# One 24-row read of a channel-attention kernel as two reads, of 123 and of 5 partitions

## The chip, the cores and the metric

The kernel runs on one core of a Trainium2 chip. The metric is the time of one execution on the device in microseconds (us). The time before is the median of three runs, 725.32 us (725.16 to 725.88).

## The reference

The input x has 384 x 384 pixels with 384 channels in bf16. The kernel takes the mean and the maximum of every channel over all pixels, sends both through the same small two-layer network (384 to 96 to 384), adds the two results, applies a sigmoid, and multiplies every pixel by the resulting 384 factors.

```python
xf = x.reshape(B, H * W, C)
gap = jnp.mean(xf, 1)
gmp = jnp.amax(xf, 1)
h_a = gap @ w1
h_a = h_a * (h_a > 0)
h_m = gmp @ w1
h_m = h_m * (h_m > 0)
scale = sigmoid(h_a @ w2 + h_m @ w2)
return x * scale[:, None, None, :]
```

So x has to be read once in full before the first output can be written. x has 113 MB and does not fit into the core's memory, which is why most of it is read twice.

## The kernel before, in words

**Rows.** The 147,456 pixels are dealt out over 128 partitions, 1,152 pixels to each. The kernel calls one pixel per partition a row: 768 bytes (384 channels in bf16) in each of 128 partitions. A block is a run of consecutive rows; within it each partition holds consecutive pixels, so that a read of n rows takes one contiguous piece of n x 768 bytes per partition (`rows_of`, line 110). The buffer `body` holds 280 rows, `held` five more.

**First pass.** All 1,152 rows are read by 53 reads that SyncE issues at line 371, in the order of the list `steps` (lines 222 to 256). For each read, TensorE sums the channels (`sums`, line 274) and VectorE takes the running maximum into `acc`, up to six rows at a time (`maximum`, line 340). Seven groups of 32 rows (`packed_block`, parts 0 to 6) stay in the buffer: ScalarE tests their values (lines 301 and 302), and TensorE and ScalarE pack 32 rows into the space of 24 (lines 322 to 329). The other rows of the first pass pass through the low rows of `body`, again and again: `BETWEEN` (line 57) lists, for each part, the blocks that are read after it and the place in `body` that they take. A read waits until the engines have finished with what lay in its place.

Part 4 is read as 24 rows into `homes[4]`, rows 256 to 279 of `body` (line 238, `FIRST_AT[4]` is 200), and 8 rows more (line 239). After it come the four blocks of `BETWEEN[4]`, of 34, 36, 31 and 26 rows, of which the first lies in rows 208 to 241 of `body`. Then part 5 is read, whose 24 rows lie in rows 232 to 255.

**Between the passes.** `fold` (line 352) and the transposes (line 423) reduce the maximum, the small network gives the factors, and ScalarE's sigmoid (line 431) writes them to `scale_bc`.

**Second pass.** What stayed in the buffer is multiplied at line 436 and written out by ScalarE's queue. The other rows are read again (line 529), multiplied and written (lines 445, 451 and 490), while VectorE and ScalarE unpack the packed parts (lines 468 to 487).

**Order.** The order on every engine is written out by hand (`manual_schedule`, line 197). SyncE issues all reads, ScalarE's queue all writes. The semaphores of the transfers are shared round robin among eight. The packed rows are restored without a loss if a test value (`judge`) is zero, else they are read again at the end (line 586); in the profiled execution they are not.

## Time and profile before

| what | value |
|---|---|
| median of three runs | 725.32 us |
| the profiled execution's own time | 725.41 us |
| its span, first to last instruction | 723.6 us |
| VectorE (DVE) busy | 564.1 us, 78% |
| ScalarE (ACT) busy | 349.8 us, 48% |
| TensorE (PE) busy | 184.7 us, 26% |
| moved by DMA | 305.63 MB, 422 GB/s over the span |
| share of 16 DMA engines, reads (q1) and writes (q10) | 62.3% and 36.6% |
| transfers under way at the longest: first pass, from issue to landing | 42.2 us at most, 19.8 in the median |

The page cuts the span into 40 slices of 18.1 us and gives the busy share of each engine in tenths. The DMA row is the mean busy share of the core's 16 DMA engines. An issue of a transfer is a short instruction on its queue; the transfer itself runs on the DMA engines, packet by packet, and is over at its landing, when the last of its end markers has come in. "L340" is line 340 of the kernel. The chain of waits follows the end of the execution back to what released each step.

### The profile page before, as it was taken

The numbers are of one execution on the slowest core, as the hardware profiler recorded it, in microseconds if no ns is written. First come the engines' busy times: TensorE is split into PE (matmuls) and PEld (weight loads), VectorE is DVE, ScalarE is ACT, GpSimd is POOL, SyncE is SP. The second block draws the span as 40 slices with busy tenths as digits, with TensorE's granted clock in tenths as the row PEclk, the third lists the DMA queues.
The fourth block names the chain that finished last, engine by engine and source line by source line (L and its number), as shares of the span: only waits on it lengthen the run. The fifth ranks groups of instructions, "written<-read, shape, count | busy, mean of one in ns | idle before, by whom it ended". The sixth has DMA issues, their size and how long they took to land.

```text
span 723.6 us, 3882 instructions
## 1 busy us (share of the span) xinstructions
PE 184.7 (26%) x1363; PEld 74.2 (10%) x1363; DVE 564.1 (78%) x445; ACT 349.8 (48%) x251; POOL 0.7 (0%) x6
## 2 busy tenths in 40 slices
PE   5577475965867470000000000000000000001000
PEld 1222122322322140000000000000000000001000
DVE  5699899999999998797966554897888889495200
ACT  6999999997999200056230023806154442200000
POOL 0000000000000000000000000000000000000000
PEclk9888878896988555555555555555555555555555
DMA  9999999999999979999999999999999999999997
GB/s 380 434 438 435 417 442 427 429 430 432 431 426 428 426 312 356 400 433 431 433 431 431 434 428 431 434 430 435 430 429 432 437 432 430 430 433 439 442 426 339
DMA packets 20403, 305.63 MB, mean 422 GB/s; under 512 B 2624, under 2 KB 2976, under 8 KB 7200
## 3 DMA queue, kind: packets, MB, share of 16 engines
q1 hardware_dynamic: 13040, 192.14, 62.3%
q10 hardware_dynamic: 7344, 113.25, 36.6%
q8 instruction: 10, 0.16, 0.1%
q14 instruction: 9, 0.07, 0.0%
HBM read 192.14 MB, written 113.25 MB: 422 GB/s over the span
## 4 chain that ended last, share of the span: by engine, by line
DMA 63%; DVE 25%; issue 3%; PE 2%; ACT 1%; SPq 0%; DVEq 0%; ACTq 0%
DMA rows<-in_x_dram 40%; DMA out_dram<-rows 23%; DVE acc L340 16%; DVE rows L436 9%; PE words_ps L322 1%; ACT rows L328 0%; DVE acc L436 0%; SPq L371 0%; PE bank_a L274 0%; ACT rows L329 0%; ACT rows L487 0%; PE bank_a L430 0%; ACT scale_bc L431 0%; DVE small L424 0%; PE bank_a L423 0%
## 5 line engine op out<-in xcount | busy, mean ns | idle before, releaser
L436 DVE TENSOR_TENSOR rows<-rows,scale_bc 128x9216 bf16<-128x9216 bf16 (+9 forms) x56 | 230.9, 4164 | 91.2 <-DMA rows<-in_x_dram 90.0
L340 DVE TENSOR_TENSOR acc<-acc,rows 128x2304 bf16<-128x2304 bf16 (+4 forms) x227 | 245.0, 1154 | 13.9 <-DMA rows<-in_x_dram 13.6
L487 ACT COPY rows<-rows 128x1536 uint8<-128x1536 uint8 x28 | 41.3, 1476 | 204.2 <-DVE rows L436 144.8
L274 PE MATMUL bank_a<-rows,small 128*1 128x512 bf16 (+3 forms) x897 | 93.3, 466 | 80.9 <-DMA rows<-in_x_dram 76.1
L346 PE MATMUL words_ps<-ident_bf,acc 128*128 128x128 bf16 x24 | 2.7, 310 | 376.3 <-DVE acc L574 376.3
L301 ACT ACTIVATE rows<-rows 128x3072 uint8<-128x3072 int8 (+1 forms) x35 | 81.9, 2341 | 9.1 <-DMA rows<-in_x_dram 8.4
L302 ACT ACTIVATE rows<-rows 128x3072 uint8<-128x3072 uint8 (+1 forms) x35 | 82.0, 2344 | 1.1
L487 ACT COPY rows<-acc 128x1536 uint8<-128x1536 uint8 x42 | 60.5, 1473 | 18.2 <-DVE acc L473 17.7
L274 PEld LDWEIGHTS <-small 128*1 128x1 bf16 x897 | 30.6, 95 | 140.3 <-issue 118.2
L346 PEld LDWEIGHTS <-acc 128*128 128x128 bf16 x24 | 2.5, 144 | 376.7 <-DVE acc L574 376.7
L322 PE MATMUL words_ps<-rows,scale_bc 128*128 128x512 fp8e4 (+1 forms) x126 | 37.9, 414 | 9.2 <-ACT rows L329 9.2
L328 ACT COPY rows<-rows 128x1536 uint8<-128x1536 uint8 x28 | 39.7, 1468 | 0.4 <-PE words_ps L322 0.4
L322 PE MATMUL words_ps<-rows 128*128 128x512 fp8e3 (+1 forms) x126 | 35.8, 394 | 0.0
L468 DVE TENSOR_SCALAR rows<-rows 128x1536 uint16<-128x1536 uint16 x56 | 31.3, 560 | 1.9
L322 PE MATMUL words_ps<-rows,w_sb 128*128 128x512 fp8e3 x84 | 27.0, 405 | 0.0
L487 ACT COPY acc<-rows 128x1536 uint8<-128x1536 uint8 x14 | 20.5, 1466 | 0.0
L329 ACT ACTIVATE rows<-words_ps 128x1536 uint16<-128x1536 f32 x14 | 20.1, 1439 | 0.0
L322 PEld LDWEIGHTS <-scale_bc 128*128 128x128 bf16 x126 | 12.2, 103 | 30.2 <-issue 19.3
L322 PEld LDWEIGHTS <-rows 128*128 128x128 bf16 x126 | 12.9, 102 | 16.7 <-issue 3.3
L473 DVE SCALAR_TENSOR_TENSOR acc<-acc,rows 128x768 uint32<-128x768 uint32 x14 | 13.4, 959 | 0.5
L473 DVE SCALAR_TENSOR_TENSOR rows<-rows 128x768 uint32<-128x768 uint32 x14 | 13.4, 958 | 0.5
L284 ACT COPY w_sb<-bank_a 65x128 f32<-65x128 f32 x2 | 0.5, 261 | 24.5 <-PE bank_a L274 24.0
(61 smaller groups left out, 72.0 us busy)
## 6 DMA issues: line engine op xcount, KB each, us to landing
rows<-in_x_dram SPq DMA_DIRECT2D x16, 2880.0 KB, 25.4
out_dram<-rows ACTq DMA_DIRECT2D x15, 2880.0 KB, 22.8
rows<-in_x_dram SPq DMA_DIRECT2D x15, 2304.0 KB, 20.0
out_dram<-rows ACTq DMA_DIRECT2D x14, 2304.0 KB, 21.1
rows<-in_x_dram SPq DMA_DIRECT2D x4, 3072.0 KB, 31.8
out_dram<-rows ACTq DMA_DIRECT2D x2, 4608.0 KB, 46.7
rows<-in_x_dram SPq DMA_DIRECT2D x9, 768.0 KB, 16.7
rows<-in_x_dram SPq DMA_DIRECT2D x2, 3264.0 KB, 26.4
```

Source lines behind the costliest of these rows:

```text
L274: nc.tensor.matmul(sum_ps[q * QP:q * QP + 1, 0:g * P], lhsT=ones_bf[:, 0:1], rhs=rows[:, k:k + g, q * P:(q + 1) * P], start=(done + k == 0 ...
L301: nc.scalar.activation(out=out_, in_=rows, func=ACT.Square, bias=test_bias, scale=TEST_SCALE)
L302: nc.scalar.activation(out=out_, in_=out_, func=ACT.Square, bias=minus4, accum_out=tests[:, k:k + 1],)
L322: nc.tensor.matmul(words[:, c:c + BANK], lhsT=weights[2 * r + k], rhs=high(part(i, r), dt)[:, half * n + c:half * n + c + BANK], start=(r ...
L328: nc.scalar.copy(out=high(part(i, r), U8)[:, span], in_=low(part(i, r + 2), U8)[:, span])
L329: nc.scalar.activation(out=part(i, 2).rearrange("p n c -> p (n c)").bitcast(U16)[:, span], in_=words, func=ACT.Copy, bias=32767.5,)
L340: nc.vector.tensor_tensor(out=out_, in0=in0, in1=in1, op=ALU.max)
L346: nc.tensor.transpose(out=out_[:, r, q * P:(q + 1) * P], in_=rows[:, r, q * P:(q + 1) * P], identity=ident_bf)
L436: nc.vector.tensor_tensor(out=dst, in0=src, in1=scale_bc.unsqueeze(1).to_broadcast([P, n, C]), op=ALU.mult)
L468: nc.vector.tensor_scalar(out=u16(dst), in0=u16(src), scalar1=s1, scalar2=s2, op0=op0, op1=op1)
L473: nc.vector.scalar_tensor_tensor(out=u32(v), in0=u32(v), scalar=0x3F3F3F3F, in1=u32(m), op0=ALU.bitwise_xor, op1=ALU.bitwise_xor)
L487: nc.scalar.copy(out=dst, in_=src)
```

## The change

The first read of part 4, the 24 rows at `FIRST_AT[4]`, is issued as two reads of the same 24 rows: one of partitions 0 to 122, one of partitions 123 to 127. They go to the same place in `body` from the same place in x. All other reads keep a single issue of 128 partitions, and what the engines do with the rows stays as it was.

```diff
+UNEVEN, FIRST_PARTITIONS = 4, 123
...
         _, block, rows, lo, hi = st
         m = hi - lo
-        nc.sync.dma_start(out=rows, in_=rows_of(xr, block)[:, lo:hi, :])
+        parts = (0, P)
+        if block == packed_block and lo == FIRST_AT[UNEVEN]:
+            parts = (0, FIRST_PARTITIONS, P)
+        for a, b in zip(parts, parts[1:]):
+            nc.sync.dma_start(out=rows[a:b], in_=rows_of(xr, block)[a:b, lo:hi, :])
         if nth < len(loads) - SUM_TAIL:
             sums(rows, m, done, TOT - tail_rows)
```

## The prediction

> **What bounds the kernel now.** I read the busy share by slices first, then the table by stretches, then the chain of waits, then a narrow window of the DMA queues for the time of one packet.

> ```profile
> DMA  9999999999999979999999999999999999999997
> GB/s 380 434 438 435 417 442 427 429 430 432 431 426 428 426 312 356 400 433 431 433 431 431 434 428 431 434 430 435 430 429 432 437 432 430 430 433 439 442 426 339
> ```

> The DMA engines are full in all but two slices (about 260 to 280 us, between the passes). The table by stretches says it without rounding; the last two columns are DMA share and GB/s.

> ```profile
> 120.00:140.00 20.00, 12.88 (x99) 4.90 (x101) 18.89 (x18) 19.42 (x13) 0.00 (x0) 0.83 1.00 426
> 140.00:160.00 20.00, 15.78 (x117) 6.41 (x110) 20.00 (x20) 19.81 (x14) 0.00 (x0) 1.00 1.01 433
> ...
> 220.00:240.00 20.00, 13.56 (x96) 5.11 (x96) 19.71 (x20) 19.82 (x15) 0.00 (x0) 0.76 1.01 430
> 240.00:260.00 20.00, 10.76 (x76) 3.14 (x76) 19.13 (x20) 0.19 (x1) 0.00 (x0) 0.50 1.01 425
> 260.00:270.00 10.00, 8.43 (x95) 6.13 (x95) 9.93 (x11) 0.95 (x4) 0.00 (x0) 0.50 0.69 268
> 270.00:280.00 10.00, 2.41 (x38) 1.69 (x34) 7.82 (x12) 0.83 (x3) 0.00 (x0) 0.50 0.76 265
> ```

> From 120 to 260 us the share is 0.99 to 1.01: no DMA engine has time to spare in the rest of the first pass. VectorE is nearly full too (18.9 to 20.0 of 20), so the chain of waits changes sides:

> ```profile
> 102.06 24.16 DMA rows<-in_x_dram
> 126.21 0.03 issue
> ...
> 164.08 20.67 DMA rows<-in_x_dram
> ...
> 230.38 11.09 DMA rows<-in_x_dram
> 241.47 0.03 issue
> ```

> At 126.2, 184.8 and 241.5 VectorE stood waiting for a landing. So up to 241.5 it has no backlog that a pause could work off to the kernel's gain; what comes after (small reads, folds, the scale) follows that landing at a fixed distance. A DMA engine that is late in the first pass makes the kernel as late.

> The time of a packet, from the window 134:136 us, inside the read in question:

> ```profile
> DMA packets 46, 0.85 MB, mean 424 GB/s; under 512 B 0, under 2 KB 0, under 8 KB 0
> ...
> q1 hardware_dynamic: 46, 0.85, 98.6%
> ```

> 46 packets took 98.6% of 16 engines times 2 us: 0.686 us each. A packet is the 18,432 B (24 rows of 768 B) of one partition. The page's second line of queues counts 2,624 packets under 512 B: 384 are the pieces of w1, and the other 2,240 are 16 end markers for each of 140 transfers. So each transfer runs on all 16 engines, 8 of 128 partitions on each (6 of w2's 96).

> **The change, part by part.** In the order of the built instructions SyncE has one more; nothing else moves, apart from semaphores that go round one further.

> Removed: one 128-partition read, 8 x 0.686 = 5.49 us of every engine.

> Added, first: one more issue on SyncE, 0.33 to 0.56 us by line 371's rows. The split read is issued at 109.45 and lands 29.6 us later, so that time lies under the queue; uncovered it costs 0.4 us. Behind it stands the 8-row read (landing after 30.9 us), covered as well.

> Added, second: 123 partitions. Every transfer of this trace is cut into 16 equal shares of whole partitions. 123 = 3 x 41 has no such cut; the largest number of engines up to 16 that takes equal shares is 3, with 41 partitions each. [...] The three engines then have 41 x 0.686 = 28.1 us, and 0.7 us more for a partition of the other read: 28.8 us in place of 5.5, **+23.3 us**, if a packet keeps its time.

> Does it? While the three engines work on it, the other thirteen have the next five reads of the queue: 8, 34, 36, 31 and 26 rows, all issued by 142.9 us into rows that reads ahead of the split one leave free. That is 135 rows at 5.49/24 = 0.229 us, 30.9 us of work. Those thirteen write to their own partitions, and the three now write to the same ones at the same time. No row shows two engines on the same partitions. From below: 0.686 us holds for packets of this size in reads and writes alike (median of both directions in the packet records), as if the engine alone set the pace. From above: both halve, 1.37 us. The longest single packet of this size took 1.18 us. I take half pace for as long as the thirteen have work, since each group of 8 partitions receives 26.9 GB/s from its one engine in all full stretches, never more, and the core's 442 GB/s at most is 16 times 27.6: I see no headroom for a second writer. Then 30.9 us bring 15.4 us of the work, the other 13.4 us run at full pace: 44.3 us in place of 5.5, **+38.8 us**. Half pace to the end: 57.6 in place of 5.5, +52.1.

> [...]

> Does the queue run dry behind it? The next read after those five waits until VectorE has passed the 34-row block (it lies over the same rows of the buffer). When the three engines end the split read, they have the 8 and 34 rows next (9.6 us), then VectorE needs 34 x 0.215 = 7.3 us (245.0 us for about 1,141 rows in line 340's group); the issue comes at 17 us, and 36 + 31 + 26 rows keep the engines to 30.9 us. Not dry; all that follows keeps its spacing, carried by the three late engines.

> A small credit: the transfer before the last stretch of the chain lands with its last marker at 241.47, while the middle of its 16 markers is near 239.7. A late trio need not hold the slowest engine; the last of three drawn from these markers is at about 240.2. **-1.3 us** (0 to -3.2).

> Sum against the profiled execution, 725.41 us (span 723.6 and 1.8 around it), and 0.09 above the median of the runs: 725.3 + 38.8 - 1.3 = **763 us**. The second pass, after the fixed distance, is shifted whole.

> **The rivals.**
> - Three engines, but each keeps 0.686 us: 725.3 + 23.3 - 1.3 = 747 us. For it: the packet time is the same in every full stretch. Against: no stretch has two engines on the same partitions.
> - Not slower: the transfer is dealt out unevenly over all 16 engines, fifteen with 8 partitions and one with 3, and the five others go to five engines. For it: all 140 transfers have 16 markers. Against: all have multiples of 16. If the short engine is the late one, it gains 5 x 0.686 = 3.4 us and the landing at 241.47 moves to its next marker, 240.2: -1.2 us; if not, one packet more on the late one: +0.7. So 724 to 726 us. It decides as soon as 14 or more engines carry the read (at most 9 partitions each, one over the 8 of before). That the split does nothing is the same case.
> - One engine takes the whole: 123 x 0.686 = 84.4 in place of 5.5: 804 us. For it: an equal cut into a power of two exists for 123 only as 1.
> - The delay is hidden, since reads are issued 20 to 30 us ahead: this speaks against itself, as the queue is FIFO work for engines that are 100% busy, so a longer queue hides no work. I count it with the even deal.

> **Chances.** Half pace 0.45; own pace 0.35; even deal or hidden 0.12; one engine 0.04; something else, slower, 0.04. The range 745 to 777 takes the first two with their bounds (747 less 1.9 for the markers' spread, 725.3 + 52.1 at the top) and leaves the even deal and the one engine out. A measurement of this kernel can tell about 0.2% (1.5 us) from no change: faster 0.03, same 0.09, slower 0.88.

> **What the profile after would show.** Right: DMA share falls to 3/16 = 0.19 from about 133.5 + 31 = 165 us until the next issue, at about 133.5 + 44.3 + 17 = 195; VectorE idle until the landing; the 123-partition read lands some 39 us later after its issue than the 29.6 of before; packets of 18,432 B with 1.37 us among them; the second pass as long as before. Own pace: a hole of half that length (to 133.5 + 28.8 + 17 = 179), a landing 23 us later, and all packets at 0.686. Even deal: no hole, both reads landing about 30 us after issue. Wrong in the step on the queue: the hole repeats further on. Wrong in the step on the end: the time between the last landing and the first multiply changes from its 7.9 us (268.3 to 276.2).

## The result, and the profile after

The changed kernel takes 776.51 us (median, 776.03 to 777.27) beside 725.54 us for the kernel before (four runs, one more than the 725.32 above rests on): 1.0704 times as long (95% interval 1.0685 to 1.0722), 51.0 us more. Its profiled execution took 776.03 us, with a span of 774.2 us. In its profile the read of line 371 is L377 and the running maximum of line 340 is L342.

The same rows of the page as before, and the line of packet counts:

```profile
DMA  9999999998499799699999999999999999999998
GB/s 383 438 424 432 438 430 400 222 218 207 166 391 429 322 402 426 252 396 419 435 432 428 434 434 428 428 431 433 432 434 430 433 433 433 430 433 435 436 432 348
DMA packets 20395, 305.63 MB, mean 395 GB/s; under 512 B 2616, under 2 KB 2968, under 8 KB 7192
```

Packets under 512 B were 2,624 and are 2,616. Sixteen end markers of the read are gone, and eight have come: 3 for the read of 123 partitions and 5 for that of 5. So the shares are as the prediction has them. What it did not have stands in the first two rows together: for three slices (of 19.4 us here, 135 to 194 us) the DMA engines are 9, 9 and 8 tenths busy and move half as much. The table by stretches of the changed kernel (last columns: DMA share, GB/s):

```profile
110.00:130.00 20.00, 11.29 (x82) 4.29 (x83) 18.63 (x18) 19.80 (x15) 0.00 (x0) 0.76 1.00 432
...
142.00:180.00 38.00, 0.00 (x0) 0.00 (x0) 0.86 (x1) 0.00 (x0) 0.00 (x0) 0.50 1.00 217
180.00:187.00 7.00, 0.00 (x0) 0.00 (x0) 0.00 (x0) 0.00 (x0) 0.00 (x0) 0.50 1.03 220
190.00:205.00 15.00, 12.08 (x83) 4.84 (x84) 12.59 (x12) 14.79 (x10) 0.00 (x0) 0.91 0.22 92
215.00:255.00 40.00, 25.64 (x195) 9.71 (x192) 38.52 (x36) 35.75 (x25) 0.00 (x0) 0.84 1.00 413
```

All sixteen engines are busy from 142 to 187 us, and together they move 217 GB/s in place of 432: all at half their pace, not the three alone (of the packets over 4 KB that start from 142 to 187 us, none moved over 16 GB/s, in the median 13.4; from 110 to 130 us it was 27.0). Then three engines are left with their backlog (share 0.22, 92 GB/s; 3/16 would be 0.19 and 81), until the next reads come. The end markers of the reads behind tell the same: of the sixteen of the 34-row read 13 come by 153.2 us and 3 from 197.8 us on, and of the 26-row read, the last in the queue, 13 by 192.2 us and 3 from 219.0 us on. VectorE meanwhile:

```profile
129.75 13.11 DVE L342 TENSOR_TENSOR acc<-acc,rows 128x2304 bf16<-128x2304 bf16 x12
190.15 6.97 DVE L342 TENSOR_TENSOR acc<-acc,rows 128x2304 bf16<-128x2304 bf16 x7 [47.29 <-DMA rows<-in_x_dram]
```

It stands for 47.3 us, for the rows of the one split read. The chain of waits shows the same gap, but under another name:

```profile
135.70 7.16 DVE acc L342 x7
142.86 47.17 another core or an unknown queue
190.15 3.77 DVE acc L342 x4
```

No other core is there. The rows came with the read of 123 partitions (three markers, the last at 188.79 us) and that of 5 (five markers, the last at 190.03 us); elsewhere in this trace a read has sixteen. That the profile leaves the wait without a name for want of markers is likely, but not shown.

From here the delay only travels. The landing at 241.47 us before is at 291.64 (+50.2), the last landing of the pass 318.63 for 268.33 (+50.3), the first multiply 326.6 for 276.2 (+50.4), and from there to the end it is 447.6 us for 447.4.

### The profile page after: what moved, and what is told of

Its sections match the earlier page's. It is cut to its first block, busy times and chain, and to the rows that moved or that the text cites. A ratio compares the mean times of both kernels' runs of the same rounds, so it can differ in the third digit from the quotient of the medians.

```text
span 774.2 us, 3883 instructions
## 1 busy us (share of the span) xinstructions
PE 184.2 (24%) x1363; PEld 73.8 (10%) x1363; DVE 564.3 (73%) x445; ACT 349.9 (45%) x251; POOL 0.7 (0%) x6
## 4 chain that ended last, share of the span: by engine, by line
DMA 59%; DVE 24%; another core or an unknown queue 6%; PE 3%; issue 2%; SPq 0%; ACT 0%; DVEq 0%; ACTq 0%
DMA rows<-in_x_dram 40%; DMA out_dram<-rows 20%; DVE acc L342 15%; DVE rows L442 8%; PE bank_a L276 2%; PE words_ps L324 1%; DVE acc L442 0%; DVE kept_ps L400 0%; DVE rows L474 0%; SPq L377 0%; PE bank_a L436 0%; ACT scale_bc L437 0%; DVE acc L474 0%; DVE bank_b L401 0%
## 5 line engine op out<-in xcount | busy, mean ns | idle before, releaser
L342 DVE TENSOR_TENSOR acc<-acc,rows 128x2304 bf16<-128x2304 bf16 (+4 forms) x227 | 245.1, 1154 | 64.3 <-DMA rows<-in_x_dram 64.0
L276 PE MATMUL bank_a<-rows,small 128*1 128x512 bf16 (+3 forms) x897 | 96.2, 478 | 132.5 <-DMA rows<-in_x_dram 127.7
L479 DVE SCALAR_TENSOR_TENSOR acc<-acc,rows 128x768 uint32<-128x768 uint32 x14 | 13.4, 959 | 0.5
L479 DVE SCALAR_TENSOR_TENSOR rows<-rows 128x768 uint32<-128x768 uint32 x14 | 13.4, 958 | 0.5
```

Source lines behind the costliest of these rows:

```text
L276: nc.tensor.matmul(sum_ps[q * QP:q * QP + 1, 0:g * P], lhsT=ones_bf[:, 0:1], rhs=rows[:, k:k + g, q * P:(q + 1) * P], start=(done + k == 0 ...
L342: nc.vector.tensor_tensor(out=out_, in0=in0, in1=in1, op=ALU.max)
L479: nc.vector.scalar_tensor_tensor(out=u32(v), in0=u32(v), scalar=0x3F3F3F3F, in1=u32(m), op0=ALU.bitwise_xor, op1=ALU.bitwise_xor)
```

## The experiments

Theories: **shares** (a read goes to the largest number of engines up to 16 that divides its partitions), **places** (an engine that writes outside the partitions it serves in a 128-partition read is slowed, and slows others), and as their rival **the cut** (two reads for one, or a piece of few partitions, cost by themselves). Times stand beside those of the kernel before, measured on the same chip.

### Cuts of the same read at 112, at 112 and 123, at 120, at 64

```diff
-            parts = (0, FIRST_PARTITIONS, P)
+            parts = (0, 112, 128)        # or (0, 112, 123, 128), (0, 120, 128), (0, 64, 128)
```

> The same read cut at 112 instead of 123: 112 and 16 partitions, which both cut into 16 equal shares (7 and 1). Theory of shares (a read goes to the largest number of engines up to 16 that divides its partitions): no engine gets more than its 8 packets, 725.5 us, within 1 us. Theory of places on top of it (a read whose shares lie on other partitions than those of a 128-partition read halves the pace of all engines while it runs): 5.5 us of work takes 11, about 731 us. Rival, the cut itself is what costs (two reads into one buffer, the last partitions apart): about 776 us as after the change.

> The cut at 123 is kept, but the 123 partitions come as 112 and 11, then the 5: shares of 7 on 16 engines, of 1 on 11, of 1 on 5. Theory of shares: the busiest engines get 9 packets for 8, +0.7 us, about 726 us; with the effect of places about 731 to 732. Rival, the cut at 123 costs: 776 us. Rival, each further read costs by itself: more than the 112 and 16 version by what one more issue takes (0.4 us).

> Cut at 120: 120 = 15 x 8, so by the theory of shares 15 engines with 8 packets each, then 8 engines with one more: the busiest has 9 for 8, +0.7 us, about 726 us. With the effect of places: 15 engines at half pace for their 8 packets, +5.5 to +6.2 us, about 731 to 732 us. If the number of engines had to be a power of two (8 engines with 15 packets, 10.3 us), +5 us, or +15 with the effect of places: 740 us. Cut itself: 776 us.

> Cut in the middle: 64 and 64 partitions, 16 shares of 4 each time. Theory of shares alone: 8 packets per engine as before, 725.5 us. If every group of partitions takes in no more than the 26.9 GB/s that its own engine brings, the 16 engines share the groups of one half: 11 us in place of 5.5, about 731 us. If a place effect hits all engines whatever they write, the same 731; the two are told apart by the cut at 112, where hardly any group is written by more than two engines at a time.

Measured, beside 725.73 us: 112 and 16: 732.34 us (ratio 1.0088, 1.0071 to 1.0105), +6.6. 112, 11 and 5: 731.5 (1.0077, 1.0060 to 1.0094), +5.8. 120 and 8: 733.44 (1.0106, 1.0089 to 1.0122), +7.7. 64 and 64: 732.26 (1.0110, 1.0077 to 1.0143; one of its four runs took 736.83), +6.5. The cut at 123 is in the second of them and costs a ninth of the change: the rival falls, and so does a price per further read (three reads cost no more than two). All four come near shares with places, whose working gave 5.5 to 6.2; three lie up to 1.5 us above it. The tables show it, here for 120 and 8:

```profile
120.00:131.00 11.00, 4.87 (x39) 1.67 (x39) 9.87 (x10) 10.87 (x7) 0.00 (x0) 0.69 1.01 436
132.00:146.00 14.00, 5.60 (x42) 2.14 (x40) 10.71 (x11) 6.72 (x5) 0.00 (x0) 0.78 1.00 206
148.00:165.00 17.00, 15.59 (x93) 5.93 (x88) 14.26 (x14) 16.87 (x11) 0.00 (x0) 0.83 1.01 434
```

For 14 us everything moves at 206 in place of some 435 GB/s: 14 x (1 - 206/435) = 7.4 us lost, of 7.7 measured. In the other three the same stretch has 247, 231 and 227 GB/s.

### The same read cut along its rows

```diff
-        parts = (0, FIRST_PARTITIONS, P)          # partitions a to b
+        parts = (0, 12, m)                        # rows a to b of all partitions
```

> The same read as two reads again, but cut along the rows: 12 rows and 12 rows of all 128 partitions. Theory of shares and places: each part goes to 16 engines with 8 packets of 9,216 B, into their usual partitions; only one more issue (0.4 us, hidden under a landing 30 us later) and 16 end markers are added: 725.5 us, within 1 us. Rival, two reads for one cost by themselves (the 6 to 8 us of the cuts at 112, 120 and 64): 731 to 733 us.

Measured: 725.78 beside 725.78 us, ratio 0.9997 (0.9988 to 1.0007). Two reads for one cost nothing here; what costs is the cut across the partitions (+5.8 to +7.7 us above, +51.0 at 123).

### The cut at 127, and the cut at 123 in a smaller read

```diff
-UNEVEN, FIRST_PARTITIONS = 4, 123
+UNEVEN, FIRST_PARTITIONS = 4, 127
```

```diff
-        if block == packed_block and lo == FIRST_AT[UNEVEN]:
+        if block == packed_block and lo == FOURTH_AT[UNEVEN]:   # the 8 rows that follow
```

> Cut at 127: by the theory of shares 127 partitions (a prime) go to one engine, 127 packets of 0.686 us = 87.1 us in place of 5.5 at its own pace. If every engine drops to half pace while one writes outside its usual partitions, the other fifteen's 30.9 us of queued work last 61.8 us, in which the one does 30.9 us; the rest at full pace: 118 us in place of 5.5, about 838 us. If one engine alone does not slow the others, 725.5 + 81.6 = 807 us, or some 820 if only the pairs that meet share. Rival, the cut as such costs the same wherever it lies: 776 us.

> The cut at 123 moved to the next read, of 8 rows (6,144 B per partition, 0.234 us a packet). Shares on 3 engines: 41 packets and one of the other read, 9.8 us in place of 1.9. Own pace: +8.0, about 733 us; half pace as long as it lasts, since the other thirteen's queue of 127 rows (29 us) outlasts it: 19.7 in place of 1.9, +17.8, about 743 us. If the cost were one of the cut (a fixed stall), 776 us.

Measured beside 725.58 us: 826.56 for 127 (1.1392, 1.1369 to 1.1415), +101.0; 739.34 for the 8 rows (1.0191, 1.0174 to 1.0208), +13.8.

127 lies between the expected 807 to 820 and 838, and for a reason that none of them had:

```profile
136.00:168.00 32.00, 2.90 (x29) 0.93 (x27) 6.91 (x7) 4.01 (x3) 0.00 (x0) 0.60 0.06 27
185.00:210.00 25.00, 0.00 (x0) 0.00 (x0) 0.00 (x0) 0.00 (x0) 0.00 (x0) 0.50 0.94 329
218.00:250.00 32.00, 10.60 (x60) 3.77 (x63) 8.00 (x8) 10.46 (x8) 0.00 (x0) 0.58 0.06 27
```

One engine works (0.06 = 1/16, 27 GB/s) and fifteen have nothing to do, although their next reads are due. SyncE was held up in issuing them; its view of line 377 has the longest issue, 60.8 us, where the median is 0.33:

```profile
L377 SPq DMA_DIRECT2D rows<-in_x_dram x54: 327/328/60781, 0.7 to 356.5; - x54
```

It is the one-partition read behind the 127, issued from 109.9 to 170.7 us. So the others ran beside the one engine only from about 171 to 216 us. In the packet records 27 of the engine's 128 packets of this size took over 1 us, and all 128 took 107.8 us, for 5.5 before: +102.3, near the +101.0.

The 8 rows: for 12 us within the split read the table has 226 GB/s at a share of 0.98. 42 packets in 13.8 + 1.9 = 15.7 us are 0.37 us each in place of 0.234, somewhat less than half pace (0.47, +17.8). In the packet records the read's first two dozen packets or so took 0.23 to 0.38 us, most of the later ones 0.36 to 0.5.

### Reads by themselves: how many engines, and at what pace

A kernel of its own leaves out the computation and does nothing but reads of p partitions by 24 rows into one buffer, each alone, then each ahead of four plain 128-partition reads of 24 rows; VectorE touches the rows after each stage.

```python
def alone(p):
    nc.sync.dma_start(out=body[0:p, 0:N, :], in_=big[0:p, 0:N, :])
    gate()
def beside(p):
    nc.sync.dma_start(out=body[0:p, 0:N, :], in_=big[0:p, 0:N, :])
    for k in range(4):
        nc.sync.dma_start(out=plain[k], in_=source[k])
    gate()
```

> A kernel that only reads: 24 rows (18,432 B per partition) of the first p partitions into one buffer, each read alone (the next waits until VectorE has looked at it), for p = 128, 128, 123, 64, 112, 120, 96, 122, 127; then each of none, 128, 123, 64, 112, 120, 96, 122, 125 ahead of four plain 128-partition reads of 24 rows. It leaves out the whole computation; its total time is of no use. Theory of shares, with 0.686 us per packet and some 2 us around each read: alone 128: 5.5 + 2; 123: 28.1 + 2 (3 engines); 64: 2.7 + 2; 112: 4.8 + 2; 120: 5.5 + 2 (15 engines); 96: 4.1 + 2; 122: 41.8 + 2 (2 engines); 127: 87.1 + 2 (1 engine). If a group of partitions takes in only 26.9 GB/s, 64 alone takes 5.5 + 2. Ahead of four plain reads (21.9 us alone): if pace halves only where two engines write the same group at a time, 123 gives 28 to 45 us in all with the plain reads near full pace, 350 GB/s in sum; if all engines halve as soon as one writes outside its usual partitions, as the trace after the change looks (215 GB/s on 16 engines), 123 gives about 44 us of half pace (21.9 x 2) and then the rest at full pace, some 50 us; 120, 112 and 96 then halve as well for as long as they run. Rival: the halving needs few engines with many packets each, then 112, 120 and 96 cost nothing and 122 and 125 halve.

Stretches inside the reads that run alone: 128, 123, 64, 112, 120, 122 and 127 partitions, in this order.

```profile
34.50:40.90 6.40, 0.00 (x0) 0.00 (x0) 1.00 0.96 369
43.00:71.00 28.00, 0.00 (x0) 0.00 (x0) 1.00 0.18 79
74.50:78.50 4.00, 0.00 (x0) 0.00 (x0) 1.00 1.04 221
82.50:87.50 5.00, 0.00 (x0) 0.00 (x0) 1.00 1.04 302
93.00:101.00 8.00, 0.00 (x0) 0.00 (x0) 1.00 0.94 200
116.00:157.00 41.00, 0.00 (x0) 0.00 (x0) 1.00 0.12 53
161.00:246.00 85.00, 0.00 (x0) 0.00 (x0) 1.00 0.06 27
```

The DMA share tells the engines: 3/16 = 0.19 for 123, 2/16 = 0.12 for 122, 1/16 = 0.06 for 127, 15/16 = 0.94 for 120, all for 64 and 112. The theory of shares fits every count in this table. The GB/s over the share tells the pace. One, two or three engines alone keep theirs: 79/3 = 26 GB/s, 0.686 us a packet. But 64 and 120 partitions run on 16 and 15 engines at 221 and 200 GB/s (13.8 and 13.3 an engine), half pace, with nothing else under way. That the engines of one read get in each other's way here is the author's reading; no trace shows it directly.

Ahead of four plain reads, 123 partitions (both phases):

```profile
310.00:340.00 30.00, 0.00 (x0) 0.00 (x0) 1.00 1.00 218
345.00:372.00 27.00, 0.00 (x0) 0.00 (x0) 1.00 0.20 81
```

218 GB/s on sixteen engines, then three at full pace: what the changed kernel shows, without the rest of it. The stage took 72.5 us, the sum of the expectation had some 50 (the three engines' own plain reads, 21.9 us, had been left out of it). 122 and 125 partitions halve everything too (218 and 221 GB/s); 64, 112, 96 and 120 cost 2 to 5 us more than their packets.

### Where it arises

Two more kernels of this kind, with other transfers ahead of the four plain reads: reads of a few partitions that stay in one group (the eight partitions that one engine is taken to serve in a read of 128), writes, copies within the on-chip memory, copies from the far memory, where x lies, to itself.

```python
for first in ((), (read, 0, 123, 24), (read, 64, 67, 96), (read, 64, 68, 96), (read, 0, 3, 96),
              (read, 0, 127, 24), (write, 0, 128, 24), (write, 0, 123, 24)):     # then four plain reads
for first in ((read, 0, 123, 24), (level, 0, 123, 24), (strided, 12, 109, 48, 96), (strided, 12, 109, 96, 96),
              (read, 0, 41, 24), (read, 0, 82, 24), (read, 0, 121, 24), (read, 0, 126, 24),
              (inside, 0, 128, 24), (inside, 0, 123, 24), (outside, 0, 123, 24)):  # likewise
```

> A kernel that only moves data, stage by stage (each stage ends when VectorE has touched all its rows); it leaves out the whole computation and its total time is of no use. Four plain 128-partition reads of 24 rows come behind: nothing; 123 partitions of 24 rows; 3 partitions (64 to 66) of 96 rows; 4 partitions (64 to 67) of 96 rows; 3 partitions (0 to 2) of 96 rows; 127 partitions; writes of 128 and of 123 partitions. Then the 123 write alone, the 64 to 66 read alone, and four plain writes behind a read of 128, a read of 123, a write of 123. Theory of local meeting: the 96-row read of 64 to 66 slows only the three engines that carry it and the one whose partitions these are; the other twelve stay at 0.686 us. Theory that everyone halves: all sixteen show about 1.3 us per packet while it runs. Alone, three engines into one group of partitions: 221 KB at 26.9 GB/s, 8.2 us, or 2.7 us if a group takes in three engines at once. 127 beside plain reads: one engine out of place halves all (about 1.3 us on all packets) or only its current partner. Writes: if the meeting is where data enters the on-chip memory, 123-partition writes (and a 123-partition read beside plain writes) leave all packets at 0.686 us; if it lies in the engines or in the far memory, the halving is there in both directions.

> Again a kernel that only moves data; it leaves out the whole computation and its total time is of no use. Ahead of four plain 128-partition reads of 24 rows stand, one stage after the other: a 123-partition read as before; one whose source lies in one piece (partition after partition) in place of 172 KB apart; 96 rows of the three partitions 12, 60, 108 (three groups, each with one visiting engine that stays there); 96 rows of the two partitions 12 and 108; reads of 41, 82, 121 and 126 partitions; copies within the on-chip memory of 128 and of 123 partitions; a copy of 123 pieces from the far memory to the far memory. Theory of shares: 41 on 1 engine, 82 on 2, 121 on 11, 126 on 14. What halves all engines beside the 123-partition read: if it is where the visitors write, the copy inside the chip halves them too and the far-to-far copy leaves them at 0.686 us; if it is the far memory's side, the other way round; if the 172 KB steps of the source do it, the read from one piece is harmless. If visitors that stay in one group each slow only their own group's engine, the three-partition read leaves thirteen engines at 0.686 us and three at 1.3 to 1.4; if two or more visitors are enough wherever they stay, all sixteen show 1.3. The 41-partition read, one engine for 28 us, then slows only the one engine that it meets, and 82, 121 and 126 slow all.

First kernel: stretches beside nothing, beside partitions 64 to 66, 64 to 67, 0 to 2, and beside the write of 123.

```profile
45.00:62.00 17.00, 0.00 (x0) 0.00 (x0) 1.00 1.00 429
144.00:150.00 6.00, 0.00 (x0) 0.00 (x0) 1.00 0.96 98
...
180.00:187.00 7.00, 0.00 (x0) 0.00 (x0) 1.00 1.00 87
217.00:222.00 5.00, 0.00 (x0) 0.00 (x0) 1.00 1.01 313
410.00:420.00 10.00, 0.00 (x0) 0.00 (x0) 1.00 0.98 418
```

Packets do not name their engine. That partitions 64 to 66 lie in one group, and 12, 60 and 108 in three, is a premise of the expectations that no trace shows directly; the packet times are measured. Below, a visitor is an engine that writes into a group that another one serves. The read of partitions 64 to 66, three visitors by the theory of shares, brings the sixteen together down to under a quarter (98 GB/s beside 429): of the 30 plain packets that lie wholly between 143.0 and 151.4 us, 22 took 2.9 us. With partitions 64 to 67, four visitors, it is a fifth (87 GB/s; 24 of 25 took 3.4 or 3.5 us). The local theory, twelve engines at full pace, falls. Beside partitions 0 to 2 the plain packets go on at 0.7 to 0.9 us (313 GB/s); the reading that the engine which serves them is itself one of the three, so that no plain read meets them, is not shown. Beside the 127 partitions one engine worked alone again, from 250 to 275 us (0.06, 27 GB/s). A write of 123 partitions leaves the reads at full pace (418 GB/s), and so does the read of 123 beside plain writes (612 of 635 packets at 0.7 us). Of writes beside writes 65 packets took 1.4 us and 534 took 0.7; that the 65 are those that meet is not shown. The read of partitions 64 to 66 alone took 7.6 us in the packet records for 221 KB, 29 GB/s, about what one engine moves (26.9).

Second kernel: beside 123 partitions, 123 from a source in one piece, three and then two partitions that stay (12, 60, 108; 12, 108), 41, 82, the copy inside of 123.

```profile
45.00:75.00 30.00, 0.00 (x0) 0.00 (x0) 1.00 1.01 216
120.00:150.00 30.00, 0.00 (x0) 0.00 (x0) 1.00 1.01 218
192.00:195.00 3.00, 0.00 (x0) 0.00 (x0) 1.00 1.00 209
222.00:226.00 4.00, 0.00 (x0) 0.00 (x0) 1.00 0.97 212
255.00:270.00 15.00, 0.00 (x0) 0.00 (x0) 1.00 0.99 392
325.00:350.00 25.00, 0.00 (x0) 0.00 (x0) 1.00 1.00 220
505.00:540.00 35.00, 0.00 (x0) 0.00 (x0) 1.00 1.01 219
```

The source does not matter (216 and 218), nor that it is far memory (the copy inside: 219). The copy from far to far, which writes nothing on the chip, left 609 of 628 packets at 0.7 us. So in these two kernels all were slowed only where both the read or copy ahead and the plain reads write into the on-chip memory (87 to 220 GB/s). Partitions 12 and 108, two visitors that each stay in a group of their own, are enough to halve all (212); one visitor is not (41 partitions: 392, and 24 of 468 packets at 1.4 us). Two in the same group do less (313), as the next kernel shows. 121 and 126 partitions, by the theory of shares on 11 and 14 engines, slowed a part of the packets only (stages of 43.9 and 34.7 us): the expectation that they slow all was wrong.

### Why the others fall back too

> A kernel that only reads; it leaves out the whole computation and its total time is of no use. Ahead of four plain 128-partition reads stand, one stage each: 128 and 123 partitions of 24 rows; 96 rows of partitions 64 to 66, of 64 and 65, of 64 alone (cut by the compiler into 16 pieces), of 0 and 1; 41 partitions of 24 rows. First with all reads on SyncE's queue, then the same with the four plain reads on ScalarE's; last, 123 partitions behind four plain reads. If what slows all engines is that they wait for descriptors in one queue, then on two queues the plain reads keep 0.686 us wherever they do not meet a visitor; if it is the way into the on-chip memory, both halves look the same: 1.3 us beside 123 partitions, 2.9 us (four writers to a group) beside 64 to 66, 2.1 us (three writers) beside 64 and 65. With partition 64 alone, 16 pieces on one group: 74 KB at 26.9 GB/s, 2.7 us, in which the plain reads nearly stand.

> A kernel that only moves data; it leaves out the whole computation and its total time is of no use. The question left open is why engines that meet no visitor fall back together with the one that is met. Ahead of four plain 128-partition transfers of 24 rows stand a read of 128 partitions, of 123, 96 rows of partitions 64 to 66, 96 rows of 12 to 14, and a copy of 48 rows inside the chip for partitions 64 to 66; in the first half the plain transfers are reads from the far memory, in the second half copies inside the on-chip memory, whose sources lie in the same partitions as their targets. If the engines are coupled through the far memory's read side (a stalled write holds up data that others wait for), the second half shows the met engine alone slowed (about 1.4 us beside 123, 2.9 beside 64 to 66) and the others near their pace of the stage behind 128; if they are coupled where they write, all are slowed in both halves. 12 to 14 should look like 64 to 66 in both.

In the first of these two, the plain reads stand on SyncE's queue and then on ScalarE's (`plain(k, nc.sync)`, `plain(k, nc.scalar)`); in the second, they are reads and then copies inside the chip (`in_=body[...]`). The first: beside 64 to 66 on one queue and on two, beside 123 on two queues, and 123 behind the plain reads.

```profile
147.00:153.00 6.00, 0.00 (x0) 0.00 (x0) 1.00 1.15 123
432.00:438.00 6.00, 0.00 (x0) 0.00 (x0) 1.00 0.93 160
375.00:395.00 20.00, 0.00 (x0) 0.00 (x0) 1.00 1.00 282
620.00:635.00 15.00, 0.00 (x0) 0.00 (x0) 1.00 1.01 433
```

Two queues soften it (282 in place of 218 GB/s, packets of 0.9 to 1.1 us where 1.3 was expected) and do not lift it, so neither expectation was met. The stages beside partitions 64 and 65, two visitors in one group, say more about how far it reaches. On one queue:

```profile
183.00:188.00 5.00, 0.00 (x0) 0.00 (x0) 1.00 1.00 313
```

From 182.6 to 189.3 us three plain packets, one right behind the other, took 2.15, 2.34 and 2.20 us, as had been expected (2.1) of an engine that meets both visitors; nearly all others of that time took 0.7 to 0.9 us. So two visitors in one group slow three packets that much and the others little, while three there brought most to 2.9 us (22 of 30, in the first kernel of the section above). Behind the plain reads the 123 costs them nothing (433 GB/s); that the others are through by the time that the three engines come to the 123 is the author's reading. The second, beside 123 partitions, plain reads and then plain copies:

```profile
80.00:110.00 30.00, 0.00 (x0) 0.00 (x0) 1.00 1.02 223
...
290.00:320.00 30.00, 0.00 (x0) 0.00 (x0) 1.00 1.00 215
```

Copies whose sources lie on the chip are halved just the same (215 GB/s, beside 395 behind a read of 128): the coupling needs no plain read from the far memory. Partitions 64 to 66 and 12 to 14 look alike, as expected, and beside both the slowest packets took 2.8 to 3.0 us in the reads and in the copies. What couples all sixteen engines, why one visitor does not do it and two in separate groups do, why two in the same group hardly do it and three do, and why 11 or 14 do it less, stays open.

## Why the prediction was right, and where it was short

The time lies in the range (745 to 777), at its very top, and 13.5 us above the predicted 763. That top was half pace to the end, for which the prediction gave no cause; that the time stayed just under it is to this extent luck.

- *Equal shares, 3 engines with 41 packets and one more*: an estimate when it was made, as the trace before has only transfers with 16 markers. Now shown, by the markers (3 and 5), by the shares of 0.18 alone and of the later backlog, and by the counts 122, 127 and 120.
- *Half pace*: shown as a pace, in the packet records of the change: 126 packets of this size from 131.5 to 189.2 us, 1.35 us in the mean. The reason given, two writers to one group with no headroom, is not shown and can be only part of it: it would slow the met engines, and here all were slowed (217 GB/s on sixteen). The rival at own pace (+23.3) is the price of the read where nothing else runs, 28 us in its own stage, and not of this kernel.
- *For as long as the thirteen have work, 30.9 us*: the step that failed. It let the thirteen go on at full pace, ready at 165 us, and the three return to 0.686 us. The thirteen were halved too; their last markers came up to 192.2 us, after the split read's last, and so the three never came back to full pace within it. The term is half pace to the end, 57.6 us in place of 5.5, which the prediction kept as its upper bound (+52.1). Measured, the last marker of the split rows comes at 190.03 us, that of the same rows before the change at 139.01: +51.0.
- *The queue does not run dry behind it*: right for the three engines that count; the hole of the others lies at 190 to 205 us, 0.22, where 165 to 195 had been given for the shorter split read. The next issue came at 206.8 us, 16.8 us after the split rows, where 17 had been worked out.
- *The late engines need not be the slowest, -1.3*: of the right size, -0.8: 51.0 at the split read, 50.2 at the landing that ended the last long wait before (241.47 us). The chain after ends its last one at an earlier read's landing, 278.82 us, so this credit is not shown by itself.
- *Fixed distance to the first multiply, second pass shifted whole*: right, 8.0 us for 7.9, and 447.6 for 447.4.
- *Rivals*: the even deal over sixteen engines and the single engine fall by the markers; the single engine is what 127 partitions give.
- *The extra issue is free*: shown by the cut along the rows, 0.0 us.
- *All but two slices, about 260 to 280 us*: misread. The row before has a 7 in one slice between the passes, 253 to 271 us, and in the very last one. No term of the sum rests on it.

## What to carry to other kernels

Cut a read along its rows (0.0 us here), not along its partitions (+5.8 to +101.0 us); if partitions have to be cut, look first at their greatest divisor up to 16 (3 engines for 123 here, one for 127), and then at whether the cut still deals them out as a whole read does (64 and 64 have sixteen engines each and cost 6.5 us). When a table shows full DMA engines at half the GB/s (1.00 and 217 here), ask not how many bytes are under way but which reads run beside each other, and of which partitions. A price for one part of the engines, worked out beside others "at full pace", needs the price of those others as well: here that was a quarter of the whole loss.
